# Attention beside a gated unit on one core: pacing of the side work, sums of out tiles on GpSimd, and planner rules of the last 13 blocks

## The chip, the cores and the metric

The kernel runs on one core of one Trainium2 chip. The metric is the device time of one execution in microseconds (us). Five runs of the kernel before took 792.3 us in the median (791.95 to 792.97).

## The reference

One input x of 2048 tokens by 640 features feeds two branches, and their product is added to x:

```
xn = layernorm(x)
q, k, v = (xn @ wqkv), split in 32 heads of 20
s = softmax(q k^T / sqrt(20)) v, heads joined, @ wo       # full attention, no mask
h = sigmoid(xn @ w_gate) * (xn @ w_up)                    # 640 -> 1728
g = silu(h @ w_down)                                      # 1728 -> 640
out = x + s * g                                           # bf16
```

The bulk is the softmax: 32 heads x 2048 x 2048 exponentials.

## The kernel before

**Blocks and tiles.** Attention is cut into 32 blocks: 8 groups of 4 heads times 4 chunks of 512 queries. A block has 64 score tiles (4 heads times 16 key tiles of 128 keys), each 128 x 512. A score tile is one TensorE matmul (`score_mm`, L977). There are two ways from a score to a probability. On ScalarE one ACTIVATE (L176) takes the exponential of one to four tiles that lie side by side in PSUM and writes them to `pu`. On VectorE a tile becomes an int16 (`iv`, L1383), and for four such tiles together three passes (L1081, L1084, L1087) make two bf16 tiles `pb`, whose sum, after the matmul, stands for the exponential. A PV round (L1029) multiplies up to four of these tiles, one per head, with v, and the four share the array. A block's sums, its row of denominators included, stand in one PSUM bank.

**After a block.** `norm_a` copies the bank to `on` on VectorE (L1043) and sends the denominators through DRAM (L1045, L1047); `norm_b` takes the reciprocal (L1053) and spreads it over the partitions with DMAs (L1055, L1058); `norm_c` multiplies (L1066), on GpSimd for all blocks but block 30, whose L1066 is on VectorE. The result of block 30 goes by four DMAs (L1070) to a tile called `o6`. All these DMAs are in the one queue of SyncE.

**Side work.** Everything else is cut into items: the projections, the gated unit's gate, up and down products (L750, L788), and the out tiles. An out tile (`mk_out`, one for 128 tokens and one half of the features) has five matmuls (L847), a VectorE product that leaves PSUM (L854, to `otmp`), a sum (L858, on VectorE or GpSimd), and, after the second half, a store issued by SyncE (L860).

**The planner.** The order of PE, ACT and DVE is not left to a scheduler. A Python loop walks through modelled time in steps of 0.01 us with durations written in the file (such as `T_F`, `T_PV`, `T_IV`), and emits an instruction when its engine is free and its inputs are ready; what it emits is the program order of each engine. A fill (F) writes scores for one exponential and up to two VectorE tiles. Two things steer it. `due()` says how much side work should be done by now; while less is done, side items may use all four free banks. `PLAN` has one row of 23 rule values for each half block (64 rows): how urgent a fill is, how many PV tiles must be ready, when VectorE may take tiles of the next block, the order of banks, and so on.

**The end.** After the last PV round of block 31: `e_on` copies the bank on ScalarE (L1126), `e_tr` transposes on PE (L1130), `e_scale` divides on VectorE (L818, L820), `e_back` transposes back (L1139), `e_o` copies on ScalarE (L1143). Then eight matmuls of `early` (L1117) multiply `o6` with its rows of wo, and eight of `late_mm` (L1121) add block 31's. VectorE and GpSimd finish (L1163 to L1174), and four stores end the kernel. PE takes the remaining out tiles, L1139, L1117 and L1121 in this order and waits in order.

Of the kernel before, what the change touches and what calls it, by code (L numbers as in the profile page):

```python
# [31 lines left out]
LEAD, M_END = 40.0, 0.6  # L32
# [46 lines left out]
    (0.25, 4, 0.15, 0, 1.2, 0.2, 1.0, 1, 8.0, 2, 3, 3, 2, 1, 4, 48, 0, 1, 14, 8, 1, 1, 0),  # L79
    (0.25, 4, 0.15, 0, 1.2, 0.2, 1.0, 1, -2.0, 2, 3, 3, 2, 1, 3, 48, 0, 1, 20, 8, 1, 0, 0),  # L80
    (0.25, 4, 0.15, 0, 1.2, 0.2, 1.0, 1, -2.0, 2, 3, 4, 2, 1, 4, 48, 0, 1, 28, 8, 1, 0, 0),
    (0.25, 4, 0.15, 0, 0.5, 0.2, 1.0, 1, -2.0, 2, 3, 4, 2, 1, 4, 48, 0, 1, 28, 8, 1, 0, 0),
    (0.25, 7, 0.15, 0, 1.2, 0.2, 1.0, 1, -2.0, 2, 3, 3, 2, 1, 3, 48, 0, 1, 20, 8, 1, 0, 0),
    (0.25, 4, 0.15, 0, 0.5, 0.2, 1.0, 1, -2.0, 2, 3, 4, 2, 3, 4, 48, 0, 1, 28, 8, 1, 0, 0),
    (0.25, 7, 0.15, 0, 1.2, 0.2, 1.0, 1, -2.0, 2, 3, 3, 2, 1, 3, 48, 0, 1, 20, 8, 1, 0, 0),
    (0.25, 7, 0.15, 0, 1.2, 0.2, 1.0, 1, 4.0, 2, 3, 3, 2, 1, 3, 48, 0, 1, 20, 8, 1, 0, 0),
    (0.25, 7, 0.15, 0.5, 1.2, 0.2, 1.0, 1, -2.0, 2, 3, 3, 2, 1, 3, 48, 0, 1, 20, 8, 1, 0, 0),
    (0.25, 3, 0.15, 0.5, 1.2, 0.2, 1.0, 1, 4.0, 2, 3, 3, 2, 1, 3, 48, 0, 1, 20, 8, 1, 0, 0),
    (0.25, 3, 0.15, 0, 1.2, 0.2, 1.0, 1, -2.0, 2, 3, 3, 2, 1, 3, 48, 1, 1, 20, 8, 1, 0, 0),
    (0.25, 3, 0.15, 0.5, 1.2, 0.2, 1.0, 1, 0.0, 2, 3, 3, 2, 1, 3, 48, 0, 1, 28, 8, 1, 0, 0),  # L90
    (0.3, 3, 0.15, 0, 1.2, 0.2, 1.0, 1, 0.0, 2, 3, 3, 2, 1, 3, 48, 0, 1, 28, 8, 1, 0, 0),
    (0.3, 3, 0.15, 0, 1.2, 0.2, 1.0, 1, 0.0, 2, 3, 3, 2, 1, 3, 48, 0, 1, 28, 8, 1, 0, 0),
    (0.3, 3, 0.15, 0, 0.35, 0.2, 1.0, 1, 0.0, 2, 3, 3, 2, 1, 3, 48, 0, 1, 28, 8, 1, 0, 0),
    (0.3, 3, 0.15, 0, 0.35, 0.2, 1.0, 1, 0.0, 2, 3, 3, 2, 1, 3, 48, 0, 1, 28, 8, 1, 0, 0),
    (0.3, 3, 0.15, 0, 1.2, 2.4, 1.0, 1, 0.0, 2, 3, 3, 2, 1, 3, 48, 0, 1, 28, 8, 1, 0, 0),
    (0.3, 2, 0.15, 0, 1.2, 2.4, 1.0, 1, 0.0, 2, 4, 3, 2, 1, 3, 48, 0, 1, 28, 8, 1, 0, 0),
    (0.3, 3, 0.15, 0, 1.2, 2.4, 1.0, 1, 0.0, 2, 4, 2, 2, 1, 3, 48, 0, 1, 28, 8, 1, 0, 0),
    (0.25, 3, 0.15, 0, 1.8, 2.4, 1.0, 1, 0.0, 2, 4, 2, 1, 1, 3, 48, 0, 1, 28, 8, 1, 0, 0),
    (0.45, 3, 0.15, 0, 1.2, 2.4, 1.0, 1, 0.0, 2, 4, 2, 2, 1, 3, 48, 0, 1, 28, 8, 1, 0, 0),
    (0.25, 4, 0.15, 0.2, 0.2, 0.2, 0.4, 1, 0.0, 2, 4, 0, 0, 2, 4, 48, 1, 1, 20, 8, 1, 1, 0),  # L100
    (0.25, 3, 0.15, 0, 1.8, 2.4, 1.0, 1, 0.0, 2, 4, 2, 1, 1, 3, 48, 0, 1, 28, 8, 1, 0, 0),
    (0.25, 4, 0.15, 0.2, 0.2, 0.8, 0.4, 1, 0.0, 2, 4, 3, 0, 2, 4, 48, 1, 1, 20, 8, 1, 1, 0),
    (0.25, 3, 0.15, 0, 1.8, 2.4, 1.0, 1, 0.0, 1, 4, 2, 1, 1, 3, 48, 0, 1, 28, 8, 1, 0, 0),
    (0.25, 3, 0.15, 0, 1.8, 2.4, 1.0, 1, 0.0, 1, 4, 2, 1, 1, 4, 48, 0, 1, 28, 8, 1, 0, 0),
    (0.25, 3, 0.15, 0, 1.8, 2.4, 1.0, 1, 0.0, 1, 4, 2, 1, 1, 3, 32, 0, 1, 28, 8, 1, 0, 0),
    (0.3, 3, 0.15, 0, 1.8, 2.4, 0.7, 1, 0.0, 1, 4, 2, 1, 1, 3, 32, 0, 1, 28, 12, 1, 0, 0),
    (0.3, 3, 0.15, 0, 1.8, 2.4, 0.7, 1, 0.0, 1, 4, 2, 1, 1, 3, 32, 1, 1, 28, 16, 1, 0, 0),
)

PRO = (  # L110
# [35 lines left out]
def kernel(  # L146
# [323 lines left out]
    def misc_ps():  # L470
        return bank[got_bank[0]]
# [42 lines left out]
    NBLK = NG * NQC  # L514
# [10 lines left out]
    def blk(g, c):  # L525
        return g * NQC + c if g < NG - 2 else PAIR + 2 * c + g - (NG - 2)

    NJOB = GH * TT
# [7 lines left out]
    def mark(*e):  # L536
        return lambda t: ev_at.__setitem__(e, t)
# [297 lines left out]
    def pool_hold(t):  # L835
        pool_from[0] = max(pool_at[0], t)
        pool_at[0] = pool_from[0] + 0.82

    def mk_out(tt, h, at):
        st = {}  # L840

        def alloc():
            st["ps"] = misc_ps()

        def mm(kd):
            hs = slice(h * HD, (h + 1) * HD)
            nc.tensor.matmul(st["ps"][:, 0:HD], lhsT=o_mid[:, kd, tt % 4 * P:(tt % 4 + 1) * P], rhs=wo[kd][:, hs],  # L847
                             start=(kd == 0), stop=(kd == KD - 1))

        def ev():  # L850
            xr, gqr = out_tiles[tt]
            sl = slice(h * HD, (h + 1) * HD)
            tmp = w2.tile([P, HD], FP32, tag="gqs", bufs=3, name="otmp")
            nc.vector.scalar_tensor_tensor(out=tmp, in0=st["ps"][:, 0:HD], scalar=0.25,  # L854
                                           in1=gqr[:, sl], op0=ALU.mult, op1=ALU.mult)
            st["v"] = n_left[NBLK - 1] <= (NJOB // 2 if h == 1 else NJOB // 4)
            add = nc.vector if st["v"] else nc.gpsimd
            add.tensor_tensor(out=xr[:, sl], in0=tmp, in1=xr[:, sl], op=ALU.add)  # L858
            if h == 1:
                nc.sync.dma_start(out=out2[tt * P:(tt + 1) * P, :], in_=xr)  # L860
        def done(t):
            mark("o", tt, h)(t)
            if st["v"]:
                late_dve[0] = 0.42
            else:
                pool_hold(t)
        return Item([("PE", alloc, [(0.136, lambda kd=kd: mm(kd)) for kd in range(KD)]),
                     ("DVE", 0.40, ev, "free", done)], at, need=blk(NG - 1, tt // 4),
                    pre=[("oc", tt // 4), ("ol", tt)])

# [67 lines left out]
    n_left = {b: TT * GH for b in range(NBLK)}  # L938
    claimed = [0]
    head_blk = [0]  # L940

    def base():
        while head_blk[0] < NBLK - 1 and not n_left[head_blk[0]]:
            head_blk[0] += 1
        return head_blk[0]
# [234 lines left out]
    with tc.manual_schedule(engines={ENG.PE, ENG.Activation, ENG.DVE}):  # L1180
# [10 lines left out]
        dq = []  # L1191
        nfill, nexp = 0, 0
        iv_left = []
        dcur = None
        dve_pass = []
# [11 lines left out]
        def progress():  # L1207
            return min(claimed[0] / NJOB, base() + 0.99)

        total = sum(x.work for x in items + glu_items)  # L1210
        done = 0.0

        def due():
            return total * min(1.0, progress() / (NBLK - M_END))

        def can_fill(f):
            if claimed[0] < NJOB * NBLK or cur is not None:
# [27 lines left out]
        while chain or timed or gos or items or glu_items or any(it.i < len(it.ops) for it in active):  # L1245
# [166 lines left out]
            if dcur is not None and claimed[0] == NJOB * NBLK:  # L1412
                if dcur["n"] == len(dcur["jobs"]):
                    dve_pass.append(dcur)
                dcur = None
# [8 lines left out]
            if free["PE"] <= now:  # L1424
# [19 lines left out]
                if cur is None:  # L1444
                    own = nfill % 2
                    m_new, m_bank = None, None
                    m_it = next((e for e in active if e.i < len(e.ops) and e.ops[e.i][0] == "PE" and e.ready <= now), None)
                    if m_it is None:
                        behind = done < due() + rule["lag"] or base() >= NBLK - 2
                        for f in M_BANKS[rule["mord"]][0:rule["mfew"] if not behind and claimed[0] < NJOB * NBLK and not (  # L1450
                            rule["fall"] and not pv_ok and not can_f) else 4]:
                            if flex[f] <= now and not (rule["excl"] and pv_bank[0] is not None and pv_ok):
                                m_bank = f
                                break
                        if m_bank is not None:
                            m_it = next((x for x in items[:80] if x.at <= progress() and (
                                x.need is None or o_at.get(x.need, 1e9) <= now) and all(
                                ev_at.get(e, 1e9) <= now for e in x.pre)), None)
                            if m_it is None and glu_items and done < due() + LEAD and all(
                                    ev_at.get(e, 1e9) <= now for e in glu_items[0].pre):  # L1460
                                m_it = glu_items[0]
                            m_new = m_it
                    m_ok = m_it is not None
                else:
                    m_ok = True
# [16 lines left out]
                if nxt == "F":  # L1482
# [3 lines left out]
                    while len(d_new) < rule["dmax"] and (dcur is not None or buf_free(iv_left, NIV)) \  # L1486
# [7 lines left out]
                        if dcur is None:  # L1494
                            iv_left.append([1, 0.0])
                            dcur = dict(jobs=[], n=0, k=0, i=len(iv_left) - 1,
                                        iv=w2.tile([P, GH, QC], I16, tag="iv", bufs=NIV, name="iv"))
                        flex[f] = 1e9
                        if d_new and d_new[-1][0] is dcur and F_POS[d_new[-1][3]] == F_POS[f] + 1:
                            p = d_new[-1]  # L1500
# [4 lines left out]
                        if len(dcur["jobs"]) == GH:  # L1505
                            dcur = None
# [95 lines left out]
```

## Time and profile before

| what | value |
|---|---|
| median of 5 runs | 792.3 us |
| the profiled execution's own time | 792.3 us |
| its span in the profile | 790.5 us |
| PE, DVE, ACT busy | 756.0, 770.3, 768.6 us |
| POOL (GpSimd) busy | 81.6 us |
| score tiles on ACT, on DVE | 1556, 492 |
| exponentials (L176 to `pu`) | 691 |
| last exponential ends | 775.44 us |

The times in the trace count from the span's start. The span leaves out 1.8 us of the execution's own time. The last row comes from the timeline of ScalarE; 775.44 us is called T below, and later events are given as T + so much.

A busy ScalarE record overlaps the next one by some tenths of a us, so a group's mean is more than the step from one to the next. From the records one by one, an exponential of two tiles ends 0.917 us after the one before, one of three tiles 1.343 us: 0.426 us a tile and 0.065 us an instruction.

### The profile page before, as it was taken

To read this page: it belongs to the slowest core of one execution; us is meant where nothing else is said; L and a number is where in the kernel's file an instruction comes from. 1 tells how busy PE (TensorE), PEld (TensorE's weight loads), DVE (VectorE), ACT (ScalarE), POOL (GpSimd) and SP (SyncE) were. 2 spreads that over 40 slices of the span, in tenths; PEclk is the share of its full clock that TensorE was granted. 3 is DMA by queue.
4 is the path that set the end of the run, shared out by engine and by line. 5 is a ranking of instruction groups with operands and counts; after the bars stand their busy time and mean duration, and the time that the engine had idled before them with its cause. 6 is when DMAs were issued, how large, how long until landed. Compare 5 with 4: busy or idle time off the path is not lost.

```text
span 790.5 us, 17148 instructions
## 1 busy us (share of the span) xinstructions
PE 756.0 (96%) x6509; PEld 272.2 (34%) x6509; DVE 770.3 (97%) x1277; ACT 768.6 (97%) x831; POOL 81.6 (10%) x98
## 2 busy tenths in 40 slices
PE   6899999999999999999999999999999999999995
PEld 5523223343333323334332333333333323333332
DVE  7899999999999999999999999999999999999998
ACT  7899999999999999999999999999999999999992
POOL 6100000000100000000000000000000001303141
PEclk9999999999999999999999999999999999999999
DMA  6521212124122132331122223334122321423312
GB/s 170 153 72 48 70 53 54 50 62 108 57 74 60 42 88 74 84 88 51 44 60 86 58 84 87 94 101 115 53 67 77 91 73 37 143 95 115 96 60 72
DMA packets 95875, 62.61 MB, mean 79 GB/s; under 512 B 36388, under 2 KB 89684, under 8 KB 95792
## 3 DMA queue, kind: packets, MB, share of 16 engines
q1 hardware_dynamic: 95504, 61.18, 27.2%
q8 instruction: 51, 0.84, 0.4%
q10 hardware_dynamic: 288, 0.33, 0.1%
q14 instruction: 32, 0.26, 0.1%
HBM read 47.84 MB, written 13.55 MB: 78 GB/s over the span
## 4 chain that ended last, share of the span: by engine, by line
ACT 52%; PE 32%; DVE 8%; issue 5%; DMA 1%; SPq 1%; DVEq 0%; ACTq 0%
ACT pu L176 47%; PE pst L977 11%; PE pst L750 7%; PE pst L1029 6%; PE pst L788 4%; ACT tnh L176 3%; DVE iv L1383 2%; DVE pb L1087 2%; ACT td L176 1%; PE pst L847 1%; PE pst L610 1%; PE pst L884 1%; DVE xn L384 0%; DMA qD<-qu 0%; ACT xnT L396 0%
## 5 line engine op out<-in xcount | busy, mean ns | idle before, releaser
L176 ACT ACTIVATE pu<-pst 128x1024 bf16<-128x1024 f32 (+2 forms) x691 | 735.3, 1331 | 1.7 <-PE pst L977 1.5
L1383 DVE TENSOR_SCALAR iv<-pst 128x512 int16<-128x512 f32 x492 | 326.0, 684 | 5.5 <-PE pst L977 3.1
L977 PE MATMUL pst<-q,kT 32*128 32x512 bf16 x2048 | 270.5, 383 | 14.5 <-ACT pu L176 9.8
L1029 PE MATMUL pst<-pu,v 128*21 128x512 bf16 x1556 | 177.9, 382 | 0.3 <-ACT pu L176 0.2
L977 PEld LDWEIGHTS <-kT 32*128 32x128 bf16 x2048 | 82.4, 91 | 255.4 <-issue 244.0
L1029 PE MATMUL pst<-pb,v 128*21 128x512 bf16 x984 | 152.6, 382 | 0.4 <-DVE pb L1087 0.4
L1087 DVE TENSOR_TENSOR pb<-iv,pb 128x2048 bf16<-128x2048 bf16 x123 | 150.8, 1226 | 0.5
L750 PE MATMUL pst<-xnT,wgu 128*128 128x512 bf16 x520 | 143.7, 382 | 1.2 <-DVE iv L1383 0.4
L1066 POOL TENSOR_TENSOR on_bf<-on,rl 128x512 bf16<-128x512 f32 x30 | 38.4, 1280 | 632.3 <-DVE rl L1064 547.2
L1081 DVE TENSOR_SCALAR pb<-iv 128x2048 int16<-128x2048 int16 x123 | 84.9, 690 | 0.1
L788 PE MATMUL pst<-wd,hT 128*128 128x320 bf16 x448 | 84.1, 302 | 0.3
L1084 DVE TENSOR_SCALAR pb<-iv 128x2048 int16<-128x2048 int16 x123 | 84.3, 685 | 0.0
L1029 PEld LDWEIGHTS <-v 128*21 128x21 bf16 x2540 | 49.5, 91 | 84.2 <-issue 61.6
L750 PEld LDWEIGHTS <-wgu 128*128 128x128 bf16 x520 | 38.5, 97 | 62.7 <-issue 40.4
L788 PEld LDWEIGHTS <-hT 128*128 128x128 bf16 x448 | 35.6, 97 | 40.2 <-issue 29.6
L610 PE MATMUL pst<-xnT,wu 128*128 128x512 bf16 x160 | 46.3, 383 | 0.1
L176 ACT ACTIVATE tnh<-pst 128x512 bf16<-128x512 f32 (+1 forms) x56 | 45.3, 809 | 0.0
L758 DVE SCALAR_TENSOR_TENSOR hT<-tnh,pst 128x512 bf16<-128x512 bf16 x52 | 35.4, 681 | 0.2
L718 PE MATMUL pst<-wv,xnT 128*128 128x160 bf16 x280 | 26.7, 233 | 1.1 <-DVE iv L1383 0.5
L718 PEld LDWEIGHTS <-xnT 128*128 128x128 bf16 x280 | 19.5, 97 | 10.5 <-issue 9.2
L847 PE MATMUL pst<-xnT,v 128*128 128x320 bf16 x120 | 21.1, 301 | 0.5 <-DVE otmp L890 0.5
L1043 DVE COPY on<-pst 128x512 f32<-128x512 f32 x31 | 21.2, 685 | 0.3 <-PE pst L1029 0.2
(115 smaller groups left out, 348.9 us busy)
## 6 DMA issues: line engine op xcount, KB each, us to landing
rl<-rd SPq DMA_DIRECT2D x124, 64.0 KB
wgu<-in_B_w_gate_dram SPq DMA_DIRECT2D x24, 320.0 KB
wgu<-in_B_w_up_dram SPq DMA_DIRECT2D x24, 320.0 KB
gq_dram<-gqs SPq DMA_DIRECT2D x24, 160.0 KB
xnT<-gq_dram SPq DMA_DIRECT2D x10, 320.0 KB
xt<-in_A_x_dram SPq DMA_DIRECT2D x16, 160.0 KB
oD<-on_bf SPq DMA_DIRECT2D x120, 20.0 KB
wd<-in_B_w_down_dram SPq DMA_DIRECT2D x1, 2080.0 KB
```

What stands on the lines that cost most here:

```text
L176: return nc.scalar.add_instruction(mybir.InstActivation(func=func, name=nc.get_next_instruction_name(), engine=ENG.Activation, ins=[nc.sca ...
L610: nc.tensor.matmul(st["ps"], lhsT=wus[u][:, kd, i, :], rhs=xnT[:, c, kd, :], start=(kd == 0), stop=(kd == KD - 1))
L718: nc.tensor.matmul(st["ps"][:, i * 2 * GC:(i + 1) * 2 * GC], lhsT=xn_tok(tts[i], kd), rhs=wvs[pr][:, kd, :], start=(kd == 0), stop=(kd == ...
L750: nc.tensor.matmul(st[key][0:fs, :], lhsT=w[:, i, kd, ko * P:ko * P + fs], rhs=xnT[:, c, kd, :], start=(kd == 0), stop=(kd == KD - 1))
L788: nc.tensor.matmul(st["ps"][:, 0:HD], lhsT=hT[0:fsz[kf], kf, t4 * P:(t4 + 1) * P], rhs=wd[0:fsz[kf], kf, h * HD:(h + 1) * HD], start=(kf = ...
L977: nc.tensor.matmul(dst, lhsT=kTs[gc(b)[0] % 2][32 * j:32 * j + 32, kt * P:(kt + 1) * P], rhs=qts[b % 3][32 * j:32 * j + 32, :], start=True ...
L1029: nc.tensor.matmul(bank[pv_bank[0]][32 * j:32 * j + DH + 1, :], lhsT=lhsT, rhs=u["src"], start=first, stop=last, tile_position=(0, 32 * j) ...
L1066: (nc.gpsimd if sync else nc.vector).tensor_tensor(out=on_bf, in0=on, in1=rl, op=ALU.mult)
L1081: nc.vector.tensor_scalar(out=pb[:, 0, :, :].bitcast(I16), in0=iv, scalar1=0x7F80, scalar2=1, op0=ALU.bitwise_and, op1=ALU.bitwise_or)
L1084: nc.vector.tensor_scalar(out=pb[:, 1, :, :].bitcast(I16), in0=iv, scalar1=0x007F, scalar2=0x3F00, op0=ALU.bitwise_and, op1=ALU.bitwise_or)
L1087: nc.vector.tensor_tensor(out=pb[:, 1, :, :], in0=iv.bitcast(BF16), in1=pb[:, 1, :, :], op=ALU.mult)
L1383: nc.vector.tensor_scalar(out=d["iv"][:, j:j + w, :], in0=pst[:, F_POS[bk]:F_POS[bk] + w, :], scalar1=B_OFF, scalar2=0.0, op0=ALU.add, op1 ...
```

## The change

1. `due()`: from progress 20 of 32 blocks on, the point by which all side work is to be done moves, over eight blocks, from block 31.4 to block 30.6.
2. `mk_out`: once every score tile is claimed and VectorE has no exponential work left in the planner's lists, the sum L858 goes to GpSimd, where before it went to VectorE.
3. `PLAN`: the 26 rows of the last 13 blocks have new values.

```
-            st["v"] = n_left[NBLK - 1] <= (NJOB // 2 if h == 1 else NJOB // 4)
+            over = claimed[0] == NJOB * NBLK and not dq and not dve_pass and dcur is None
+            st["v"] = n_left[NBLK - 1] <= (NJOB // 2 if h == 1 else NJOB // 4) and not over
             add = nc.vector if st["v"] else nc.gpsimd
...
         def due():
-            return total * min(1.0, progress() / (NBLK - M_END))
+            p = progress()
+            return total * min(1.0, p / (NBLK - M_END - 0.8 * min(1.0, max(0.0, (p - 20) / 8))))
...
-    (0.25, 4, 0.15, 0, 0.5, 0.2, 1.0, 1, -2.0, 2, 3, 4, 2, 1, 4, 48, 0, 1, 28, 8, 1, 0, 0),
+    (0.25, 4, 0.15, 0, 1.2, 0.2, 1.0, 1, 8.0, 2, 3, 4, 2, 1, 4, 48, 1, 1, 20, 8, 1, 0, 0),
...
-    (0.3, 3, 0.15, 0, 1.8, 2.4, 0.7, 1, 0.0, 1, 4, 2, 1, 1, 3, 32, 1, 1, 28, 16, 1, 0, 0),
+    (0.25, 4, 0.15, 0.2, 0.2, 0.2, 0.4, 1, 0.0, 2, 4, 0, 0, 2, 4, 48, 1, 1, 20, 8, 1, 1, 0),
```

The program order that comes out is the same up to the middle of the run, on VectorE up to its 792nd instruction (at 485 us in the profile before), and differs from there to the end. The counts of what each engine does hardly differ:

| count in the program | before | after |
|---|---|---|
| exponentials of 1, 2, 3, 4 tiles on ACT | 16, 488, 184, 3 | 10, 495, 180, 4 |
| score tiles on ACT | 1556 | 1556 |
| `iv` on DVE: single, double | 492, 0 | 490, 1 |
| L858 on DVE, on POOL | 7, 17 | 2, 22 |

The ends of the two queues that matter below, from the last pass on `pb` (L1087) on:

```
DVE before: ... L1066, L854, L858, L1081, L1084, L854, L858, L1087(last), 3 x (L854, L858), L818, L820, 2 x (L854, L858), L1163 ...
DVE after:  ... L1053, L1383, L1081, L1383, L1084, L1383, L1087, L1081, L1084, L1087(last), L854, L1066, 2 x L854, L818, L820, 2 x L854, L1163 ...
SP before:  ... L1055, 4 x L1058, 4 x L1070, L860, L860, L860, L860, L1178
SP after:   ... L860, L1055, 4 x L1058, L860, 4 x L1070, L860, L860, L1178
```

In the program after, the L860 that stands ahead of the four L1070 waits for GpSimd, for the sum of the L854 that follows the last L1087.

## The prediction

> **What bounds the kernel now.** I read the page's busy shares, then windows of the last third, then the timeline of each engine around the last exponential. Columns of the windows: length, then busy time of PE, PEld, DVE, ACT and POOL with counts, PE clock, DMA share, GB/s.
>
> ```profile
> PE 756.0 (96%) x6509; PEld 272.2 (34%) x6509; DVE 770.3 (97%) x1277; ACT 768.6 (97%) x831; POOL 81.6 (10%) x98
> ```
> ```profile
> 515.00:540.00 25.00, 23.79 (x222) 8.88 (x224) 24.16 (x42) 25.00 (x25) 1.26 (x1) 1.00 0.45 126
> ...
> 740.00:765.00 25.00, 23.72 (x208) 9.15 (x211) 24.79 (x42) 25.00 (x28) 9.53 (x10) 1.00 0.19 60
> 765.00:790.00 25.00, 17.55 (x158) 7.08 (x150) 21.62 (x39) 11.61 (x16) 3.54 (x4) 0.94 0.20 69
> ```
>
> All three large engines look full. Which of them sets the pace shows where one never waits: ACT has 25.00 of 25 in every window from 440 to 765, the changed stretch (485 us on) included, while PE and DVE miss up to 1.2 us. Records one by one say the same: the ends of all exponentials after 485 us exceed 0.426 us a tile plus 0.065 us an instruction by 0.3 us in total. So ACT is the bound up to T = 775.44, and its work is 1556 score tiles before and after.
>
> Behind T the timeline has another chain (start, length, engine, line):
>
> ```profile
> 750.24 25.20 ACT L176 ACTIVATE pu<-pst 128x1024 bf16<-128x1024 f32 x28
> 777.19 0.59 ACT L1126 COPY on<-pst 128x512 f32<-128x512 f32 x1 [1.75 <-PE pst L1029]
> 780.64 0.58 ACT L1143 COPY o<-pst 80x512 bf16<-80x512 bf16 x1 [2.86 <-PE pst L1139]
> ...
> 771.77 0.69 DVE L1066 TENSOR_TENSOR on_bf<-on,rl 128x512 bf16<-128x512 f32 x1
> ...
> 775.43 1.22 DVE L1087 TENSOR_TENSOR pb<-iv,pb 128x2048 bf16<-128x2048 bf16 x1
> ...
> 779.35 0.25 DVE L818 RECIPROCAL rq<-pst 128x16 f32<-128x16 f32 x1
> 779.64 0.49 DVE L820 TENSOR_TENSOR onq<-pst,rq 128x320 bf16<-128x320 f32 x1
> ```
> ```profile
> 777.86 0.63 PE L1130 MATMUL pst<-ident_f,on 128*128 128x128 f32 x4
> ...
> 780.18 0.42 PE L1139 MATMUL pst<-ident,onq 128*80 128x128 bf16 x4 [0.34 <-DVE onq L820]
> 780.58 0.60 PE L1117 MATMUL pst<-wo_t,o 80*128 80x128 bf16 x5
> 781.50 0.81 PE L1117 MATMUL pst<-wo_t,o 80*128 80x512 bf16 x3 [0.33 <-DVE otmp L854]
> 782.15 1.25 PE L1121 MATMUL pst<-wo_t,o 80*128 80x128 bf16 x8
> ```
> ```profile
> 767.32 1.71 SPq L1058 DMA_DIRECT2D rl<-rd  x4
> 772.49 3.11 SPq L1070 DMA_DIRECT2D o<-on_bf  x4
> 775.71 2.26 SPq L860 DMA_DIRECT2D out_dram<-xnT  x2
> ```
>
> The reader sees the last pass end at T + 1.21, e_on start at T + 1.75, the transposes end at 778.49 = T + 3.05, and L818 come only at T + 3.91, since DVE still has three pairs of L854 and L858 ahead of it. L1121 starts at T + 6.71, and the span ends 8.39 us later. One line carries no wait but matters most: the four DMAs of o6 start at 772.49, their last packet ends at 776.48 by the packet records, and L1117, which needs them, starts at 780.58. They have over 3 us of slack.
>
> **The change, part by part.** *Before T.* Two exponentials fewer at 0.065 us: -0.13 us. No other gain is to be had there, for ACT's tiles stay and its waits are 0.3 us. New rows can make it wait: not less than 0 (less than 0 is excluded by those 0.3 us); at most, by the same stretch, I take 1 us (PE and DVE have 0.2 to 1.2 us of spare in 25). Taken: 0.2, since the old rows, on engines as full, cost 0.3. The pacing and the rows together move PE and DVE work, whose sums stay (matmuls equal in number; the double iv saves DVE some tenths of a us); ACT covers them while they feed it.
>
> *The five sums moved to GpSimd.* On DVE an L858 costs 0.53 us from end to end, and three of those before ran ahead of L818, 1.6 us. Without them L818 can follow the transposes. But DVE's order now has L854, L1066, L854, L854 ahead of it. By rows: last PV round behind two matmuls, one PV round and five more matmuls of L847, so about T + 1.38 where it was T + 1.27; e_on from T + 1.87; transposes done T + 3.17; e_scale to T + 4.0; L1139 from T + 4.1, 0.65 us earlier than before; e_o done at T + 5.1. If nothing else were late, L1121 could start at T + 5.3 instead of T + 6.71.
>
> *What is late next: o6.* The last pass of VectorE is now followed by L854 and only then by L1066, which before ended 2.98 us ahead of T. When does the last pass end? From below: the last iv needs the fill issued when all but four exponentials are done, two of two tiles and two of three, 4.52 us before T; scores 0.44, iv 0.60, L1087 1.13, L1081 and L1084 0.60 each, L1087 1.13 end at T + 0.0. From above: DVE is full from the copy L1043 on; that copy follows a PV round behind the fill issued fifteen exponentials from the end, so 15.04 us before T, starts at T - 14.2, and the instructions from it to the last pass take 14.6 us; beside GpSimd's sums the same stretch of before lost 0.7 us, and another 0.5 may be behind: T + 1.6. I take T + 0.7, midway, as neither chain is seen to decide.
>
> Then, with D for that end: L854 and L1066 end at D + 1.0, or up to 0.8 later if rl is not there: L1053 ends at D - 6.4, and before 7.5 us passed from it to L1066 without a wait that shows. Behind L1066 only two L854 and L818 queue up, so this costs nothing while the store below holds SyncE as long. SyncE is not free for o6, though: the store L860 stands ahead of the four L1070 in its queue and waits for GpSimd's sum. That sum starts at D + 0.48 (GpSimd starts 0.08 us after the L890 that feeds it) and takes 0.79 us, as four of eight L892 do:
>
> ```profile
> 755.69 0.79 POOL L892 TENSOR_TENSOR wd<-otmp,xr 128x320 f32<-128x320 f32 x1 [0.43 <-DVE otmp L890]
> ```
>
> It ends at D + 1.27 (bounds 0.72, one half of L1166, and 1.24, the L858 at 764.67). The store follows 0.19 later and takes 0.36, so the first L1070 goes at D + 1.87. Its last packet ended 3.99 us after the first issue before: D + 5.86. Landing as seen by a waiting engine: the nearest row is L1058, which started 0.94 us after the last packet of the DMA it waits for; into SBUF it may be as little as 0.3. I take 0.6: D + 6.46, T + 7.16. L1117 to L1121 is 1.57 - 0.33 of wait = 1.24 us: L1121 at T + 8.44, where it was T + 6.71. That is +1.73 us. PE stands idle for some 2.5 us ahead of L1117, so the 0.65 us won on the way there is lost in that wait. The other four sums on GpSimd (four times 0.79 to 1.24 behind L854s that end by T + 5.5) are done before L1166 asks, at about T + 9.4, and the stores of their tiles stand behind o6: nothing.
>
> [...]
>
> **Sum.** -0.13 + 0.2 + 1.73 = +1.8 us on the profiled execution's 792.3 us, which is also the median: **794.1 us**, 0.23% slower. About 0.2%, 1.6 us, is what a measurement of this kernel can tell from no change, so the forecast lies just behind that edge.
>
> **Rivals.**
> - *o6 is late by little.* For it: the L1070 take 0.7 us each to issue, where L1074 and L708, of the same size, take 0.32 and 0.28; if that was chance, the last goes 1.2 us sooner; the lowest D takes another 0.7, and the quick landing 0.3. Against it: all four L1070 were slow alike. Sum: 791.9 to 793.4, no change by the bound.
> - *o6 is in time* (the other side). If SyncE's DMAs land before T + 4.2, PE goes from L1139 straight on and the shorter DVE chain counts: L1121 at T + 5.3, -1.4 - 0.13 us, 790.8, at best 790.6. It decides at a landing 3 us earlier than I reckon. For it: DVE's tail is 2.6 us shorter in program order. Against it: D cannot be under T + 0.0, and L854, the sum, the store, four issues and a landing follow it in a row.
> - *ACT starves.* The new rows hold back PV until more tiles are ready and the pace asks for more side work between blocks 20 and 28. An exponential that waits once per block for 0.15 us costs 2 us: 796 and more. For it: DVE and PE waits of up to 1.2 us in 25 in the old rows. Against it: the sums stay equal.
> - *The change does not do what it says:* counts of ACT do not move, so the rules may do nothing before T. That is contained in the forecast.
>
> **How the numbers follow.** The forecast's case (o6 late by 1 to 3 us, 793.4 to 795.5, its own range) has 0.56, of which 0.13 lies under 793.9; o6 late by little 0.22; in time 0.08, of which 0.04 is faster by over 0.2%; ACT starved 0.14, all slower. Slower: 0.43 + 0.14 = 0.57; same: 0.13 + 0.22 + 0.04 = 0.39; faster: 0.04. The range leaves out 1 in 10 below (the case in time) and 1 in 10 above: 791.9 to 796.2, the latter with the highest D (+0.9), the slow sum (+0.45) and 0.75 of more ACT waits.
>
> **What will show it.** Right: a PE wait ahead of L1117 of 2 to 3 us put down to the DMA o<-on_bf; L1066 after T instead of before it; L860 ahead of L1070 in SyncE's timeline; L818 within 0.2 us of the transposes' end; ACT idle nowhere before T; T within 0.3 us of 775.3. Wrong: L1117 right behind L1139, a T later by a us or more, or L1070 issues of 0.3 us.

## The result and the profile after

The median is 794.17 us (25 runs, 792.93 to 797.05), beside 792.24 us for the kernel before (45 runs). The ratio is 1.0025, with a 95% interval of 1.0018 to 1.0032: 0.25% slower, some 1.9 us. A second comparison of the same two kernels on another chip (e6 below) gave 1.0022 [1.0012, 1.0031]. The forecast was 794.1 us, slower by 0.23%.

The busy shares of the page of the kernel after tell nothing of it. PE and ACT are as full as before, VectorE is a little less busy, GpSimd a little more:

```profile
PE 756.9 (95%) x6509; PEld 273.4 (34%) x6509; DVE 768.3 (97%) x1271; ACT 767.9 (97%) x829; POOL 85.6 (11%) x103
```

The time lies behind the last exponential, which ends at T = 775.34 here. From L856 on the line numbers are one higher than before: L1067 is the product norm_c, L1071 the four DMAs of o6, L1118 early, L1122 late. First the timeline of PE around the end of the work (start, length, engine, line, shapes, and in brackets the idle time before it and what ended it), then PE's entry in the list of waits (total, times, longest):

```profile
777.85 0.63 PE L1131 MATMUL pst<-ident_f,on 128*128 128x128 f32 x4
778.32 1.25 PE L847 MATMUL pst<-xnT,v 128*128 128x320 bf16 x8
779.40 0.39 PE L1140 MATMUL pst<-ident,onq 128*80 128x128 bf16 x4
782.95 1.25 PE L1118 MATMUL pst<-wo_t,o 80*128 80x128 bf16 x8 [3.16 <-DMA o<-on_bf]
784.04 1.37 PE L1122 MATMUL pst<-wo_t,o 80*128 80x128 bf16 x8
```
```profile
PE pst L1118 <- DMA o<-on_bf: 3.2, 1, 3.2
```

L1140 starts at T + 4.06, where it stood at T + 4.74 before: that much was won. Then PE stands for 3.16 us until o6 has landed, and L1122 starts at T + 8.70, where late started at T + 6.71. How o6 came to be late is seen on three other engines of the same kernel, VectorE, GpSimd and SyncE's queue:

```profile
775.16 1.23 DVE L1088 TENSOR_TENSOR pb<-iv,pb 128x2048 bf16<-128x2048 bf16 x1
776.30 0.48 DVE L854 SCALAR_TENSOR_TENSOR otmp<-pst,xnT 128x320 f32<-128x320 f32 x1
776.70 0.68 DVE L1067 TENSOR_TENSOR on_bf<-on,rl 128x512 bf16<-128x512 f32 x1
777.30 1.04 DVE L854 SCALAR_TENSOR_TENSOR otmp<-pst,wd 128x320 f32<-128x320 f32 x2
778.52 0.26 DVE L818 RECIPROCAL rq<-pst 128x16 f32<-128x16 f32 x1 [0.18 <-PE pst L1131]
```
```profile
776.86 1.17 POOL L859 TENSOR_TENSOR xnT<-otmp,xnT 128x320 bf16<-128x320 f32 x1 [9.05 <-DVE otmp L854]
778.00 1.54 POOL L859 TENSOR_TENSOR wd<-otmp,wd 128x320 bf16<-128x320 f32 x2
```
```profile
771.29 1.71 SPq L1059 DMA_DIRECT2D rl<-rd  x4
778.06 0.36 SPq L861 DMA_DIRECT2D out_dram<-xnT  x1
778.51 3.10 SPq L1071 DMA_DIRECT2D o<-on_bf  x4
781.73 0.89 SPq L861 DMA_DIRECT2D out_dram<-wd  x2
```

The last pass L1088 ends at T + 1.05, L854 and L1067 follow it, and L1067 is done at T + 2.04; before it was done 2.98 us ahead of T. The sum on GpSimd, fed by that L854, ends at 778.03; the store L861 goes 0.03 us later; only then does SyncE issue the first L1071, at T + 3.18, over a microsecond after its data were ready. L818 comes 0.04 us after the transposes, since VectorE has no sums to do there any more.

### The profile page after: what moved, and what is told of

Its sections match the earlier page's. It is cut to its first block, busy times and chain, and to the rows that moved or that the text cites. A ratio compares the mean times of both kernels' runs of the same rounds, so it can differ in the third digit from the quotient of the medians.

```text
span 792.8 us, 17147 instructions
## 1 busy us (share of the span) xinstructions
PE 756.9 (95%) x6509; PEld 273.4 (34%) x6509; DVE 768.3 (97%) x1271; ACT 767.9 (97%) x829; POOL 85.6 (11%) x103
## 4 chain that ended last, share of the span: by engine, by line
ACT 52%; PE 33%; DVE 8%; issue 5%; DMA 1%; SPq 0%; DVEq 0%; ACTq 0%
ACT pu L176 45%; PE pst L978 11%; PE pst L750 7%; PE pst L1030 5%; PE pst L788 3%; DVE iv L1385 3%; ACT tnh L176 3%; PE pst L610 2%; PE pst L847 2%; DVE pb L1088 2%; ACT td L176 1%; ACT sq L372 1%; ACT xnT L396 1%; ACT sq L370 1%; DVE pb L1085 1%
## 5 line engine op out<-in xcount | busy, mean ns | idle before, releaser
L1030 PE MATMUL pst<-pu,v 128*21 128x512 bf16 x1556 | 174.2, 382 | 0.3 <-ACT pu L176 0.2
L1088 DVE TENSOR_TENSOR pb<-iv,pb 128x2048 bf16<-128x2048 bf16 x123 | 150.5, 1223 | 0.6
L1067 POOL TENSOR_TENSOR on_bf<-on,rl 128x512 bf16<-128x512 f32 x30 | 39.4, 1314 | 636.2 <-DVE rl L1065 558.2
L859 POOL TENSOR_TENSOR xnT<-otmp,xnT 128x320 bf16<-128x320 f32 x18 | 17.6, 985 | 46.7 <-DVE otmp L854 46.6
```

Of the source, the lines that this page charges most:

```text
L1030: nc.tensor.matmul(bank[pv_bank[0]][32 * j:32 * j + DH + 1, :], lhsT=lhsT, rhs=u["src"], start=first, stop=last, tile_position=(0, 32 * j) ...
L1067: (nc.gpsimd if sync else nc.vector).tensor_tensor(out=on_bf, in0=on, in1=rl, op=ALU.mult)
L1088: nc.vector.tensor_tensor(out=pb[:, 1, :, :], in0=iv.bitcast(BF16), in1=pb[:, 1, :, :], op=ALU.mult)
```

## The experiments

Ratios are to the kernel before on the same chip, with their 95% intervals. The executions that were profiled need up to 2 us more or less for the time up to the 50th exponential (82.70 to 84.66 us) with one and the same program there, so stretches are compared from its end on. The table has, for every profile, the time from there to T, and then offsets from T: the end of the last pass (D), the first issue of o6's DMAs, the starts of early and late, and the end of the span. All in us, worked out from the instruction records. What is called the 50th exponential, here and in the expectations, has 50 others ahead of it.

The chips differ a little: the kernel before takes 792.24 us in the first comparison, 793.08 beside e1 to e4, 792.58 beside e5 to e8 and 793.37 beside e9 and e10. The kernel after ran in the first comparison and beside e5 to e8 alone. By their medians e1 to e4 stand 0.4 to 1.0 us lower against before than by their profiles; why is open, and the step-by-step readings below go by the profiles.

| kernel | 50th exp. to T | D | o6 issue | early | late | end |
|---|---|---|---|---|---|---|
| before | 691.21 | 1.21 | -2.96 | 5.14 | 6.71 | 15.10 |
| after | 690.68 | 1.05 | 3.18 | 7.62 | 8.70 | 17.49 |
| e1, o6 not needed | 690.59 | 1.03 | 3.17 | 4.41 | 5.53 | 14.34 |
| e2, store out of the way | 690.54 | 1.04 | 2.06 | 6.50 | 7.58 | 16.44 |
| e3, o6 first | 690.69 | 1.51 | 0.41 | 4.85 | 5.93 | 14.73 |
| e4, two DMAs more | 690.58 | 1.04 | 5.09 | 9.40 | 11.42 | 20.25 |
| e5, before again | 691.40 | 1.21 | -2.96 | 5.14 | 6.71 | 15.10 |
| e6, after again | 690.55 | 1.05 | 3.18 | 7.62 | 8.71 | 17.50 |
| e7, before + sums on GpSimd | 693.73 | 1.21 | -2.96 | 4.50 | 5.97 | 14.36 |
| e8, after with sums on VectorE | 690.62 | 1.05 | 2.60 | 7.53 | 8.61 | 17.40 |
| e9, before + pacing | 693.37 | 1.46 | -1.70 | 5.44 | 6.53 | 15.21 |
| e10, before + rows | 694.07 | 4.53 | 0.95 | 7.94 | 10.07 | 19.08 |

**e5 and e6: both kernels once more, unchanged** (run after e1 to e4).

> The kernel before, unchanged, profiled once more beside the others. In the five profiles so far the time from the span's start to the 50th exponential varies from 82.7 to 84.7 us with the same program; from there to the last exponential it is 691.21 us before and 690.5 to 690.7 us in the changed kernel and its variants. Theory W2 (o6 costs 2.4 us behind T, the new rows win 0.6 us ahead of it): 691.2 us again, tail behind T 15.1 us again. If that 0.6 us is chance: 690.6 us here. Time: as before, ratio 1.000.

> The changed kernel, unchanged, on the same chip as the others. W2: 690.6 us from the 50th to the last exponential, tail 17.4 us, ratio 1.002 to 1.003. If the first result was high by chance, as the shorter times of the variants suggest: ratio 1.001.

Measured: 792.16 us, 0.9995 [0.9987, 1.0004], and 794.49 us, 1.0022 [1.0012, 1.0031]. The offsets behind T repeat to 0.01 us, the stretch from the 50th exponential to T to 0.2. From that exponential to the end the kernel after takes 708.17 and 708.05 us, the kernel before 706.31 and 706.50: 1.7 us more, of which -0.7 lies ahead of T and +2.4 behind it.

**e1: does o6 hold the end?** Its matmuls read a tile that has long been there. Block 30's share of the last four out tiles is left out for it.

```diff
-        nc.tensor.matmul(dst, lhsT=last["o6"][:, t4 * P:(t4 + 1) * P], ...
+        nc.tensor.matmul(dst, lhsT=kTs[0][0:GC, t4 * P:(t4 + 1) * P], ...
```

> The changed kernel, but the eight matmuls of early (L1118) read a tile of keys that is long there instead of o6. The four DMAs of o6 still run, nobody reads them; what block 30 adds to the last four out tiles is left out and replaced by other numbers. Theory W (the loss is PE's 3.16 us of waiting for o6): L1118 follows L1140 at once, e_o at about T + 5.1 is then the last input of L1122, so L1122 starts near T + 5.6 instead of T + 8.71: 3.1 us less, 791.1 us, faster than the kernel before. [...] Rival R (the new rows lose the time before T): 794.2 less the part of the wait that the rows do not explain, so not under 793.

Measured: 790.58 us, 0.9969 [0.9959, 0.9978]. PE of e1 runs on without a break:

```profile
778.51 0.39 PE L1140 MATMUL pst<-ident,onq 128*80 128x128 bf16 x4
778.86 1.28 PE L1118 MATMUL pst<-wo_t,kT 80*128 80x128 bf16 x8
779.98 1.25 PE L1122 MATMUL pst<-wo_t,o 80*128 80x128 bf16 x8
```

The end behind T is 3.15 us shorter than after's, which is the length of the wait taken away (3.16). The wait for o6 is the whole loss and more: without it the time lies below that of the kernel before.

**e2: is the store ahead of o6's DMAs at fault?** Stores that come before o6 is issued are kept and issued by ScalarE behind e_on.

```diff
...
+                if claimed[0] == NJOB * NBLK and "o6" not in last:
+                    kept.append((tt, xr))
+                else:
-                nc.sync.dma_start(out=out2[tt * P:(tt + 1) * P, :], in_=xr)
+                    nc.sync.dma_start(out=out2[tt * P:(tt + 1) * P, :], in_=xr)
...
         nc.scalar.copy(out=last["on"], in_=bank[pv_bank[0]])
+        for tt, xr in kept:
+            nc.scalar.dma_start(out=out2[tt * P:(tt + 1) * P, :], in_=xr)
```

> The changed kernel, but the one store of an out tile (L861) that stands ahead of o6's DMAs in SyncE's queue is issued by ScalarE instead, behind e_on, where ScalarE waits for L1140 anyway. Theory W: the first DMA of o6 starts right behind L1067 (ends 777.38), at 777.4 instead of 778.51, and everything behind it comes 1.1 us sooner: 793.1 us. If the late L1067 alone decides and the store does not: no change, 794.2. [...]

Measured: 793.27 us, 1.0000 [0.9990, 1.0010]. In SyncE's queue of e2 the DMAs of o6 (L1075 there) now go 0.02 us after the product, at T + 2.06, and PE's wait for them is shorter by the same 1.1 us (early is L1122 there):

```profile
775.30 3.10 SPq L1075 DMA_DIRECT2D o<-on_bf  x4
```
```profile
779.74 1.25 PE L1122 MATMUL pst<-wo_t,o 80*128 80x128 bf16 x8 [2.04 <-DMA o<-on_bf]
```

So the store's place is worth 1.05 us of the 2.4 behind T. The other part is the place of the product itself, behind the last pass.

**e3: product and DMAs of o6 ahead of the last pass instruction and of the store.** Nothing is left out.

```diff
                     k = d["k"]
+                    if k == 2 and claimed[0] == NJOB * NBLK and len(dve_pass) == 1 and not dq and gos:
+                        _, b, on, rl = gos.pop(0)
+                        norm_c(b, on, rl, False)
+                        ev_at[("o6",)] = now + 2.5
                     if k == 0:
```

> The changed kernel, but L1067 of block 30 is put ahead of the last pass (L1088) on VectorE instead of behind it and an L854; the store then stands behind o6's DMAs too. Theory W: L1067 runs at 775.15 to 775.85, provided the spread reciprocals have landed (their last packet ended at 774.17), the DMAs of o6 start at 775.9, last packet 779.9, L1118 at 780.3. The last pass ends 0.6 us later, which moves the last PV round by 0.35, to T + 1.7, L1140 to 779.75. L1122 at 781.4 instead of 784.04: 2.6 us less, 791.6 us. [...]

Measured: 791.37 us, 0.9978 [0.9967, 0.9989], faster than the kernel before, and so than the kernel after. VectorE, SyncE's queue and PE of e3:

```profile
773.57 0.68 DVE L1067 TENSOR_TENSOR on_bf<-on,rl 128x512 bf16<-128x512 f32 x1
774.17 1.22 DVE L1088 TENSOR_TENSOR pb<-iv,pb 128x2048 bf16<-128x2048 bf16 x1
```
```profile
774.28 3.10 SPq L1071 DMA_DIRECT2D o<-on_bf  x4
777.48 0.42 SPq L861 DMA_DIRECT2D out_dram<-xnT  x1
```
```profile
778.14 0.39 PE L1140 MATMUL pst<-ident,onq 128*80 128x128 bf16 x4
778.72 1.25 PE L1118 MATMUL pst<-wo_t,o 80*128 80x128 bf16 x8 [0.19 <-DMA o<-on_bf]
779.80 1.25 PE L1122 MATMUL pst<-wo_t,o 80*128 80x128 bf16 x8
```

The last pass is later by 0.46 us (D at T + 1.51), but o6 is issued at T + 0.41 and PE waits 0.19 us for it instead of 3.16. The end comes 2.76 us sooner. What the change won in the tail is to be had as soon as this one product keeps its place.

**e4: a longer queue ahead of o6.** Two more DMAs of the same size, into a spare tile, go first.

```diff
+            spare = wk.tile([P, QC], BF16, tag="aq", bufs=4, name="o6s")[0:GC, :]
+            for j in range(2):
+                nc.sync.dma_start(out=spare[j * DH:(j + 1) * DH, :], in_=on_bf[32 * j + 1:32 * j + 1 + DH, :])
             for j in range(GH):
```

> The changed kernel with two more DMAs of the size of o6's (20 rows of 1 KB, to a tile that nobody reads) issued by SyncE right ahead of the four. Theory W: each took 0.77 us of SyncE, so o6 lands 1.5 us later and the kernel takes 1.5 us more: 795.7 us. [...]

Measured: 796.56 us, 1.0044 [1.0029, 1.0058]; the end behind T is 2.76 us later than after's, where some 1.5 were expected. SyncE's queue of e4, and PE (early is L1121 there):

```profile
777.43 1.88 SPq L1072 DMA_DIRECT2D o6s<-on_bf  x2
779.35 2.96 SPq L1074 DMA_DIRECT2D o<-on_bf  x4
```
```profile
783.66 2.23 PE L1121 MATMUL pst<-wo_t,o 80*128 80x128 bf16 x8 [4.94 <-DMA o<-on_bf]
```

The issue is 1.91 us later and the wait 1.78 longer. The rest is not the queue: early's eight matmuls took 2.23 us instead of 1.25, and late's 2.34. The windows of e4 (length, busy time of PE, PEld, DVE, ACT, POOL, PE clock, DMA share, GB/s) show the granted clock fall:

```profile
782.00:783.60 1.60, 0.00 (x0) 0.00 (x0) 0.00 (x0) 0.00 (x0) 0.00 (x0) 1.00 0.25 80
783.60:785.60 2.00, 1.94 (x8) 0.95 (x9) 0.00 (x0) 0.00 (x0) 0.00 (x0) 0.54 0.33 120
785.60:788.00 2.40, 2.40 (x9) 0.88 (x7) 1.64 (x4) 0.00 (x0) 1.07 (x2) 0.50 0.00 0
```

So the longer wait cost more here than its length: with early at half clock, late starts another 0.94 us later than the wait alone explains. Late's own slowness hardly reaches the end (8.83 us from late's start to the end, 8.79 in after). My expectation left the clock out.

**e7 and e8: the sums' engine alone.** e7 is the kernel before with only the new term `over`, e8 the kernel after without it.

```diff
-            st["v"] = n_left[NBLK - 1] <= (NJOB // 2 if h == 1 else NJOB // 4)
+            over = claimed[0] == NJOB * NBLK and not dq and not dve_pass and dcur is None
+            st["v"] = n_left[NBLK - 1] <= (NJOB // 2 if h == 1 else NJOB // 4) and not over
```

> The kernel before with the second part of the change alone: sums behind the last exponential on GpSimd, old rows, old pacing. L1067 of block 30 stays 3 us ahead of T. Theory W: o6 lands at about T + 2, PE never waits for it, and three sums fewer ahead of L818 let it follow the transposes: e_scale from T + 3.1, L1140 behind ten L847 at T + 4.25, L1118 at T + 4.65, L1122 at T + 5.75 instead of T + 6.71: 1.0 us less than before, 791.3 us, ratio 0.9988. Rival P (sums on GpSimd cost time): slower than before by 0.5 us or more.

> The changed kernel without its second part: sums behind the last exponential on VectorE, as before; new rows and new pacing stay. Theory W: the store ahead of o6 now waits for VectorE's sum, which ends before L1066, so o6's DMAs follow L1066 at D + 1.55 instead of D + 2.12; L818 comes later, but inside PE's wait. 0.55 us less than the changed kernel: 793.6 us, ratio 1.0018, and a PE wait for o6 of about 1.5 to 2 us. Rival R (the rows are the loss before T): 794.2. Rival P: below 792.5.

Measured for e7: 791.34 us, 0.9984 [0.9974, 0.9993]: alone this part is a gain. Its end behind T is 0.74 us shorter; about 1.0 was expected, but early waits for VectorE once more, as PE of e7 shows:

```profile
782.55 0.60 PE L1118 MATMUL pst<-wo_t,o 80*128 80x128 bf16 x5
783.37 0.81 PE L1118 MATMUL pst<-wo_t,o 80*128 80x512 bf16 x3 [0.21 <-DVE otmp L854]
784.01 1.25 PE L1122 MATMUL pst<-wo_t,o 80*128 80x128 bf16 x8
```

(Its 693.73 us up to T hold a disturbance, told in the last section.) Measured for e8: 793.39 us, 1.0012 [1.0002, 1.0023]. The median is as expected (1.1 us under that of e6 on the same chip), the profile is not: the end behind T is only 0.09 us shorter than after's. The store no longer waits for GpSimd, so o6 is issued 0.58 us sooner, but its four DMAs took longer, 3.59 us to issue instead of 3.10, all of it in the first (1.29 us instead of 0.81; the other three 0.71 to 0.74 as in after), and PE waited on them again:

```profile
776.81 0.36 SPq L860 DMA_DIRECT2D out_dram<-xnT  x1
777.41 3.59 SPq L1070 DMA_DIRECT2D o<-on_bf  x4
```
```profile
782.33 1.25 PE L1117 MATMUL pst<-wo_t,o 80*128 80x128 bf16 x8 [1.93 <-DMA o<-on_bf]
```

One profile does not tell whether that slower issue belongs to this order or to this execution; it stays open. What holds is that the sums on GpSimd, a gain in the old order (e7), show none in the new one.

**e9 and e10: pacing alone and rows alone**, each in the kernel before.

```diff
 e9:
-            return total * min(1.0, progress() / (NBLK - M_END))
+            p = progress()
+            return total * min(1.0, p / (NBLK - M_END - 0.8 * min(1.0, max(0.0, (p - 20) / 8))))
 e10: in the table of rules, the rows of the last 13 blocks
-    (0.25, 4, 0.15, 0, 0.5, 0.2, 1.0, 1, -2.0, 2, 3, 4, 2, 1, 4, 48, 0, 1, 28, 8, 1, 0, 0),
...
+    (0.25, 4, 0.15, 0, 1.2, 0.2, 1.0, 1, 8.0, 2, 3, 4, 2, 1, 4, 48, 1, 1, 20, 8, 1, 0, 0),
...
```

> The kernel before with the first part of the change alone: the new pacing, old rows, sums as before. Its program puts 1559 instead of 1556 score tiles on ACT, in 692 exponentials instead of 691. Theory W2 (ACT sets the pace up to T): 3 tiles at 0.426 us and one instruction at 0.065 us more, 1.34 us, so 692.6 us from the 50th to the last exponential if the pacing does not shorten ACT's waits, 692.0 if it does so as in the changed kernel. L1066 ends about 2.5 us ahead of D, so o6 is not waited for; behind T about 15 us as before. 793.2 us, ratio 1.0012. A rival by which the pacing is what costs the changed kernel its time: 794 or more, ratio above 1.002.

> The kernel before with the third part alone: the new rows, old pacing, sums as before. Its program puts 1560 score tiles on ACT, in 692 exponentials. W2: 4 tiles and one instruction more, 1.77 us, less 0.6 us of shorter waits: 692.4 us from the 50th to the last exponential. No out tile is left behind the last pass, L1066 stands two passes groups ahead of it, so L818 follows the transposes and o6 is there in time or late by little: about 14.5 us behind T. 792.8 us, ratio 1.0007. Rival R (the new rows make the loss): ratio above 1.002.

Measured for e9: 794.04 us, 1.0013 [1.0000, 1.0026], the expected ratio. Its profile agrees less: the stretch up to T is 693.37 us, 0.8 longer than the top of the range given (three more tiles on ACT are in that range; one step of ACT at 745.6 us is 0.68 too long), and the end behind T is 15.21. Measured for e10: 798.47 us, 1.0070 [1.0056, 1.0085], where 1.0007 was expected: a plain miss. From the 50th exponential T comes 2.9 us later than before (four more tiles on ACT make 1.7 of it), and behind T the order falls apart. PE of e10, from the last PV rounds on:

```profile
779.81 0.40 PE L1029 MATMUL pst<-pb,v 128*21 128x512 bf16 x4 [1.08 <-DVE pb L1087]
780.41 0.40 PE L1029 MATMUL pst<-pb,v 128*21 128x512 bf16 x4 [0.21 <-DVE pb L1081]
782.27 0.40 PE L1029 MATMUL pst<-pb,v 128*21 128x512 bf16 x4 [1.46 <-DVE pb L1087]
783.40 0.85 PE L1130 MATMUL pst<-ident_f,on 128*128 128x128 f32 x4 [0.73 <-ACT on L1126]
785.19 0.65 PE L1139 MATMUL pst<-ident,onq 128*80 128x128 bf16 x4 [0.94 <-DVE onq L820]
785.63 2.34 PE L1117 MATMUL pst<-wo_t,o 80*128 80x128 bf16 x8
```

With the old pacing side work is left over: six pairs of L854 and L858 stand on VectorE ahead of the last two groups of passes, the last pass ends at T + 4.53, PE waits for passes, and early runs at half clock (0.50 from 783.7). The rows are not good or bad by themselves; they fit the pacing that they came with. Alone, the rows are slower and the pacing is not faster. Of the kernels that compute the whole result, two beat the kernel before: the three parts with o6 put first (e3), and the sums alone in the old order (e7).

## Why the prediction was right

**The mechanism** was the forecast's own: o6, which had over 3 us of slack, becomes the last thing that PE waits for. e1, e2 and e3 show it by taking the wait away, by shortening it at the store, and by moving the product. The chain, step by step, predicted and then measured: last PV T + 1.38 and + 1.36; e_on + 1.87 and + 1.85; transposes' end + 3.17 and + 3.15; L1140 + 4.1 and + 4.06; L1122 + 8.44 and + 8.70. Of the signs named ahead, all of the right ones came (the wait of 3.16 us lies just over the 2 to 3 named), and no wrong one: T is 0.04 us from 775.3, and L1071 issues took 0.77 us each. That T came so near is luck: with the same program up to there it lies between 773.24 and 775.34 in seven profiles, as the time up to the 50th exponential varies.

**Two sizes were off by 0.7 us, with opposite signs**, so the sum of +1.8 against +1.7 in the profiles is better than its parts; that it came so near is luck. Two of the forecast's additions are a little off too: 7.16 and 1.24 make T + 8.40, not 8.44, and the terms up to the first L1070 make D + 1.82, not 1.87.

- *Before T*: taken +0.07 (-0.13 and +0.2 for new waits), measured about -0.7: -0.53 in the first pair of profiles, -0.85 in the second (e5, e6). The step that failed is "no other gain is to be had there", with less than 0 excluded by the 0.3 us of waits: those were waits of the old order, and a new order can lose them. Over the first 424 exponentials, which are the same in both kernels, each takes 408.9 us from the 50th on, so the gain lies behind them. There the steps from one exponential's end to the next that exceed 0.426 us a tile plus 0.065 us an instruction by over 0.01 us add up to 0.32 us in before (five steps, the largest at 521, 533 and 698 us) and to 0.50 in e5; the kernel after and its variants (e1 to e4, e6, e8) have no such step. With 0.13 for two exponentials fewer that is 0.45 of 0.53 and 0.63 of 0.85; the rest is spread over many steps and stays open. Pacing alone and rows alone have more such waits than before, 1.1 us in e9 and 1.3 in e10, so it takes both to lose them. The double `iv`, taken to save VectorE some tenths of a us, saves it 0.06: it took 1.23 us in after, two single ones in a row 1.28 in the median of both traces.
- *Behind T*: taken +1.73, measured +2.39. Term by term: D at T + 1.05, 0.35 later than the value taken, inside its bounds. The sum on GpSimd took 1.17 us, not 0.79: +0.38, inside the bound of 1.24. The store went 0.16 sooner after it than reckoned. From o6's last packet to L1118 0.44 us passed, not 0.6, and L1118 to L1122 took 1.09, not 1.24. Together these make about the +0.26 on L1122 (8.70 against 8.44). Another +0.40 lies behind it: from the start of late to the end 8.79 us, where 8.39 was taken over from before. The kernels with the old rows and the old pacing (before, e5, e7) have 8.39 there, all others 8.68 to 9.01 (the largest is e10, with late at half clock). In after, 0.33 us of it is a gap among SyncE's last steps, behind the last work; why it is there stays open.

**The sum beside L1067.** The forecast took 0.79 us from a row of GpSimd's sums before. The sum took 1.17 us in after, where it overlaps L1067 for 0.52 us (and in e1, e2, e4 and e6, with the same order), and 0.80 in e3, where L1067 ran long before:

```profile
775.87 0.80 POOL L859 TENSOR_TENSOR xnT<-otmp,xnT 128x320 bf16<-128x320 f32 x1 [9.53 <-DVE otmp L854]
```

It took 0.37 us longer beside L1067, less than the whole overlap, and ended at D + 1.65; the row that I took gave D + 1.27. Such times stood in the trace of before already: of its 25 sums on GpSimd (L858, L892) five took 1.17 us and five 1.24 to 1.77, all ten beside one of VectorE's passes (L1081, L1084, L1087).

**The rivals.** "o6 is in time" was priced at 790.8 us, and decides, as written, at a landing 3 us earlier. e1, where PE need not wait for the landing, gives 790.58; e3 comes near it with 791.37. "ACT starves" did not come in the kernel after (ACT is busy for 25.00 of 25 us in every window from 440 to 765), but e10 shows that it was no idle fear: the same rows with another pacing lose about 1.1 us ahead of T beyond the four tiles more that ACT has there, and 4.0 behind it. "The change doesn't do what it says" falls for the sums and the rows, which move the time alone; of the pacing alone the interval just reaches 1.0000.

## What to carry to other kernels

Before an engine's queue is shortened, look at what leaves the critical path with it and what was early only because of the old order: here a 0.68 us product slid behind the last pass, a store that now waits for another engine stood ahead of its DMAs, and 3 us of slack became a 3 us wait. One product and its transfers put back in their place (e3) turned a loss of 0.25% into a gain of 0.22%. Moving the sums alone (e7) had gained 0.16%; the intervals of the two overlap, so it is not shown that the new rows and the pacing add anything to that. Rules and pacing that were chosen together are judged together: neither alone showed what the pair does ahead of T.

## What the hardware showed that was not expected

**The clock fell behind one wait and not behind another of the same length.** In e4 PE is idle from 778.7 for 4.94 us, and the granted clock is 0.50 from 783.8 on, so that early and late take 2.23 and 2.34 us, where each takes 1.25 in e2 and e3. In after PE is idle from 779.8 for 3.16 us, and the clock falls at 785.0, in the middle of L1122 (1.37 us instead of 1.25):

```profile
784.00:785.40 1.40, 1.40 (x9) 0.52 (x7) 0.94 (x3) 0.00 (x0) 0.37 (x1) 0.87 0.00 0
```

In e6, the same program with the same wait, it stays at 1.00 until 788.2, when all matmuls are done; yet both end alike, at T + 17.49 and + 17.50, so in after the fall cost nothing. In e10 short bursts of matmuls in between, 1.10 us of the 3.50 ahead of 783.5, did not hold it up: 0.50 from 783.7. The stretches at one granted clock that lie between two changes last 23.89, 3.41 and 750.93 us in after, which is 7, 1 and 220 times the shortest of them, and the one in before lasts 781.65 us, 229 times that. Over the last 3.41 us ahead of the fall PE was busy for 0.10 us in e4 and for 2.09 in after; 2.16 of 3.41 us in e6 led to none. What decides is not shown.

**A stretch at half clock with PE busy.** In e7's profile one stretch of 3.4 us has a clock of 0.50 though PE was at work just before, as the windows show; ACT, fed by PE, was busy for 2.56 of it, and most of the 2.3 us that this profile lost up to T lie there and just behind. I have no cause for it.

```profile
161.40:164.80 3.40, 2.20 (x25) 1.16 (x23) 3.40 (x8) 3.40 (x4) 0.00 (x0) 1.00 0.63 138
164.80:168.20 3.40, 3.40 (x17) 1.31 (x13) 3.21 (x5) 2.56 (x3) 0.00 (x0) 0.50 0.26 85
168.20:171.60 3.40, 3.40 (x43) 1.08 (x42) 2.48 (x5) 2.76 (x4) 0.00 (x0) 0.99 0.00 0
```

**o6's DMAs cost more to issue than those of the same rows to DRAM.** The four DMAs of o6, from SBUF to SBUF, take 0.71 to 0.82 us each to issue in every profile, but for the first in e8 (1.29). The same rows of the same tile, sent to DRAM for an earlier block by SyncE of the kernel after, take 0.35 here, and 0.32 in the median of all 120 such issues (0.27 to 1.25, so a single slow one is seen there too):

```profile
706.50 1.39 SPq L1075 DMA_DIRECT2D oD<-on_bf  x4
```

The forecast allowed that the 0.7 us of before might be chance; it was none. In the program the two differ in the destination; what makes the difference in time was not tried.
